# Turned left rows in the order (row, segment) instead of (segment, row), in a recurrent attention kernel with streamed weights

## The chip, the cores and the metric

The kernel runs on one core of a Trainium2 chip. The metric is the device time of one execution in microseconds. A core has a matrix engine (TensorE, PE in the profile, PEld for its weight loads), three engines for vector work (VectorE = DVE, ScalarE = ACT, GpSimd = POOL), and a queue engine (SyncE = SP). Transfers are carried out by 16 DMA engines; SP, ACT and POOL issue them.

## The reference

The input `x` has 2048 rows of 1024. It is normalized row by row (`xn`), and the result is `x` plus two branches. Branch A is attention with a recurrent memory, over 64 segments of 32 rows:

```
mem = mem0                                        # 8 rows
for s in range(64):
    h = concat([mem, xn[32*s : 32*s+32]])         # 40 rows
    q, k, v = h @ Wq, h @ Wk, h @ Wv              # 32 heads of 128
    p = softmax(mask(q k^T * scale))              # a key is seen from memory rows, or if it isn't later
    o = (p v) @ Wo
    mem = o[:8];  out[32*s : 32*s+32] = o[8:]
```

So the memory of a segment is made by the segment before, and the segments run one after the other. Branch B takes the two rows of `xn` with the highest score under `w_r`, sends them through a gated feed-forward layer (width 3584) and adds the result to these two rows. Data are bf16.

## The kernel before

**Weights.** Wq, Wk, Wv and Wo are cut into 64 granules of 512 KB. 44 stay in SBUF for the whole run. The other 20 are streamed anew in every segment: `fetch` (L346) issues on SP's queue, into five slots (tile `g`), from copies in DRAM (`wsc`) that the first segment makes. SP waits until TensorE has let go of a slot.

**Main rows and left rows.** A segment's tile has 32 rows. 24 of them are the segment's first 24 rows of x (XM = 24), the other 8 are the memory. The segment's last 8 rows (XL = 8, the *left* rows) do not fit. Four segments are a group `G`, and the left rows of its four segments, 4 x 8 = 32 rows, are one more tile `STL`. Their q, k and v need no memory, so they are computed for the next group while this group's segments run: each `left_pass` (L566) multiplies STL with a granule that happens to be there, into `PSl`. The places are written out by hand in `PASSES`, and the copies out of PSum in `COPIES`. Which of the 32 columns of STL is which row is the subject of the change: before it, column 8 s + r is row r of segment s.

**The way of the left rows.** `load_left` (L318) fetches them from x with four DMAs on GpSimd's queue, one for each quarter of the columns: into `XL`, `BX` (the next group's rows, normalized by `norm_left` with the statistics in `ML`) and, with `crossed`, into `OL` (the same rows again for the final sum, `sum_left`, L330). The left q and k of a group go to DRAM (`ql_d[G]`, four matrices of 128 x 512, L617 from ScalarE's queue), since each segment needs only its own quarter of the rows. `new_lx` (L481) fetches this quarter, 128 rows of 512, for the next segment, in the ninth step of the output projection (`w == 9`); `turn_lx` (L488) transposes it on TensorE behind the first transposes of the segment (L491), and ScalarE copies it into `QKL`. In the first segment `turn_first` (L497) does the same without DRAM.

**Softmax.** For each half of the heads, `soften` (L682) writes the normalized weights of the 32 main keys into PM and those of the 8 left keys into a tile with room for all 32 left rows of a group, zero at the other segments' (L704); VectorE transposes both in blocks of 32 x 32 (L706, L708), and `attend` (L712) multiplies them with VM and VL, the values of the main rows and of the left rows of the whole group. The room with zeros is slot 3 of `OTL` (`left_out`, L510) or a part of `BX`; `clear_pl` (L744) clears it with a memset on GpSimd.

**Statistics.** `spread` (L224) brings means and deviations from rows of 128 to the layouts that are needed, by matmuls with 0/1 matrices made at the start (`SELM`, `SELL`), once for the first 128 rows and once for the rest.

**Order.** The order on each engine is the order of the program (a manual schedule): hooks at (phase, step) in a segment place softmax, attend, loads and copies between the matmuls (L802 for q, k, v, L575 for the output projection).

Of the kernel before, what the change touches and what calls it, by code (L numbers as in the profile page):

```python
# [11 lines left out]
ALU = mybir.AluOpType  # L12
# [38 lines left out]
def kernel(  # L51
# [16 lines left out]
    nc = tc.nc  # L68
    P = 128
# [3 lines left out]
    SEG = int(A_seg_len)  # L73
# [4 lines left out]
    NT = S // P  # L78
# [4 lines left out]
    XM = SEG - M  # L83
    XL = M
    NK = M + SEG

    x2 = A_x[0]
# [38 lines left out]
    ql_d = [dram.tile([4, P, 512], BF16, name=f"ql_d{t}") for t in range(NT)]  # L126
# [22 lines left out]
    IDENT = const.tile([P, P], BF16, name="IDENT")  # L149
# [10 lines left out]
    BS = psS.tile([P, 512], F32, name="BS")  # L160
    BT = psT.tile([P, 512], F32, name="BT")
    SPS = BS[:, 0:8 * NK].rearrange("p (i a k) -> p i a k", i=4, a=2)
    PTB = BT[:, 0:256].bitcast(BF16)
    PTB2 = BT[:, 256:512].bitcast(BF16)
    OPB = BT[:, 256:256 + 4 * NK]
    MR = BS[:, 320:320 + 2 * NSEG].rearrange("p (s c) -> p s c", c=2)
    ML = BS[:, 448:448 + 2 * NT].rearrange("p (t c) -> p t c", c=2)
    nc.vector.memset(SPS[:, :, :, :], 0.0)
    for b in range(2):
        nc.vector.memset(X[b][:, :], 0.0)  # L170
# [3 lines left out]
    MISC = home(hm, [P, 2048], BF16, "MISC")  # L174
    SELM = MISC[:, 0:512].rearrange("p (s g r) -> p s g r", s=4, g=4)
    SELL = MISC[:, 512:640].rearrange("p (g s r) -> p g s r", g=4, s=4)
# [4 lines left out]
    RI16 = MISC[:, 728:792].bitcast(F32).rearrange("p (t c) -> p t c", c=2)  # L181
    RF = MISC[:, 792:824].bitcast(F32)
    MF = MISC[:, 824:824 + 2 * (XM + 1)].bitcast(F32)
    WRB = MISC[:, 1024:2048]
    nc.vector.memset(MF, 0.0)
    nc.vector.memset(MISC[:, 0:640], 0.0)

    for q0 in range(0, P, 32):
        for c0, c1, base, step in ((0, XM, 0, -1), (XM, XM + 1, -XM, 0)):
            nc.gpsimd.affine_select(out=MF[q0:q0 + 32, c0:c1], in_=MF[q0:q0 + 32, c0:c1], pattern=[[step, c1 - c0]],  # L190
                                    compare_op=ALU.is_ge, fill=NEG, base=base, channel_multiplier=1)
        nc.gpsimd.affine_select(out=CT[q0:q0 + 32, 14:15], in_=CT[q0:q0 + 32, 14:15], pattern=[[0, 1]],
                                compare_op=ALU.is_ge, fill=1.0, base=XM - 1, channel_multiplier=-1)
    nc.vector.tensor_scalar(out=KMSK, in0=NMSK, scalar1=-1.0, scalar2=1.0, op0=ALU.mult, op1=ALU.add)
    nc.vector.tensor_copy(out=MASK, in_=MF[:, 0:XM])
    nc.vector.tensor_copy(out=NEGR, in_=MF[:, XM:XM + 1])
    for s in range(4):
        nc.vector.tensor_copy(out=SELM[:, s, :, 0:XM],
                              in_=IDENT[:, 32 * s:32 * s + XM].unsqueeze(1).to_broadcast([P, 4, XM]))
        nc.vector.tensor_copy(out=SELL[:, s, :, :],  # L200
                              in_=IDENT.rearrange("p (s c) -> p s c", c=32)[:, :, XM:SEG])


    XP = {}
# [19 lines left out]
    def spread(t0, t1):  # L224

        n = t1 - t0
        sd_rows(MV[:, t0:t1, :], VE[:, t0:t1])
        PD = OPB
        for s in range(5):
            sel = SELM[:, s, :, :].rearrange("p g r -> p (g r)") if s < 4 else SELL.rearrange("p g s r -> p (g s r)")  # L230
            nc.tensor.matmul(PD[:, 32 * s:32 * s + 2 * n], lhsT=sel, rhs=MV[:, t0:t1, :].rearrange("p t c -> p (t c)"),
                             start=(s == 0), stop=True, skip_group_check=True)
        for s in range(4):
            mr = MR.rearrange("p (t s) c -> p t s c", s=4)[:, t0:t1, s, :]
            pd = PD[:, 32 * s:32 * s + 2 * n].rearrange("p (t c) -> p t c", c=2)
            nc.vector.tensor_copy(out=mr[:, :, 0], in_=pd[:, :, 0])
            nc.vector.tensor_scalar(out=mr[:, :, 1], in0=pd[:, :, 1], scalar1=NMSK, scalar2=None, op0=ALU.add)
        nc.vector.tensor_copy(out=ML[:, t0:t1, :], in_=PD[:, 128:128 + 2 * n].rearrange("p (t c) -> p t c", c=2))
        nc.vector.tensor_copy(out=RI16[:, t0:t1, 0], in_=MV[:, t0:t1, 0])
        nc.vector.reciprocal(out=RI16[:, t0:t1, 1], in_=MV[:, t0:t1, 1])  # L240

# [23 lines left out]
    def two_rows(m, tag):  # L265
        t = one.tile([P, 4], F32, tag=tag, name="RI")
        nc.vector.tensor_copy(out=t[:, 0:1], in_=m[:, 0:1])
        nc.vector.reciprocal(out=t[:, 1:2], in_=m[:, 1:2])
        return t
# [46 lines left out]
        nc.vector.tensor_copy(out=gview(st)[:, :, :, XM:SEG], in_=PTm[:, :, :, XM:SEG])  # L316

    def load_left(G, t, crossed=False):  # L318
        o4 = x2[4 * G * SEG:4 * (G + 1) * SEG, :].rearrange("(s r) d -> s r d", s=4)
        for g in range(4):  # L320
            b = 2 * (g % 2) + g // 2 if crossed else g
            nc.gpsimd.dma_start(out=t[32 * g:32 * (g + 1), :], in_=o4[:, XM:SEG, 256 * b:256 * (b + 1)])
        return t

    def norm_left(t, G):
        mr = two_rows(ML[:, G, :], "ri")
        nc.vector.tensor_scalar(out=t[:, :], in0=t[:, :], scalar1=mr[:, 0:1], scalar2=mr[:, 1:2],
                                op0=ALU.subtract, op1=ALU.mult)

    def sum_left(t, G):  # L330

        mr = two_rows(ML[:, G, :], "ri")
        nc.vector.tensor_scalar(out=mr[:, 0:1], in0=mr[:, 0:1], scalar1=mr[:, 1:2], scalar2=-1.0,
# [87 lines left out]
    load_x(0)  # L421
    nc.sync.dma_start(out=WRB, in_=B_w_r.unsqueeze(0).to_broadcast([P, D]))
    load_seg(0)
# [57 lines left out]
    def new_lx(s):  # L481
        t = lx[0] = one.tile([P, 512], BF16, tag="bA", name="LX")
        G, j = divmod(s, 4)
        nc.gpsimd.dma_start(out=t[:, :], in_=ql_d[G].rearrange("m (q s r) c -> (m q) s r c", q=4, s=4)[:, j])  # L484

    lx = [None]

# [9 lines left out]
    def turn_first(mat, half, XBl):  # L497
        if mat == 0 and half == 0:
            qkl[0] = one.tile([P, 4, 4, 4, XL], BF16, tag="bC", name="QKL")
        PTq = PTB.rearrange("p (i c) -> p i c", i=4)  # L500
        for il in range(4):
            nc.tensor.transpose(out=PTq[:, il, :], in_=XBl[:, il * P:(il + 1) * P], identity=IDENT[:, :])
        nc.scalar.copy(out=qkl[0][:, :, 2 * half + mat, :, :],
                       in_=PTB.rearrange("p (i q s r) -> p i q s r", i=4, q=4, s=4)[:, :, :, 0, :])

    qkl = [None]
    group = {}
# [113 lines left out]
    for s in range(NSEG):  # L621
        G, j = divmod(s, 4)
# [59 lines left out]
        def soften(half):  # L682
            S8 = SPS.rearrange("p i a k -> p (i a) k")
            DN = one.tile([P, 8], F32, tag="nm", name="DN")
            nc.vector.tensor_reduce(out=DN[:, :], in_=S8, axis=AX.X, op=ALU.add)
            nc.vector.reciprocal(out=DN[:, :], in_=DN[:, :])
            PT2 = one.tile([P, 2, 4, 64], BF16, tag=("bA", "bE")[half], name="PT2")
            PTm, PTl = PT2[:, 0], PT2[:, 1]
            PM = PTl.rearrange("p i q -> p (i q)").rearrange("p (b k) -> p b k", b=8)
            PLt = zeros_and_left()  # L690
            dnb = DN[:, :].unsqueeze(2)
            nc.vector.tensor_tensor(out=PM, in0=S8[:, :, 0:32], in1=dnb.to_broadcast([P, 8, 32]), op=ALU.mult)
            apart = half == 1 and j == 3
            if apart:
                OT[0] = one.tile([P, 640], BF16, tag="kt", name="OT")
                Z = OT[0][:, 512:640]
                nc.vector.memset(Z, 0.0)
                parts = [(slice(0, 4), Z.rearrange("p (b s r) -> p b s r", b=4, s=4)), (slice(4, 8), PLt[:, 4:8])]
                OT[0] = OT[0][:, 0:512].rearrange("p (i j r) -> p i j r", i=4, j=4)
            else:  # L700
                parts = [(slice(0, 8), PLt)]
            for bs, z in parts:
                n = bs.stop - bs.start
                nc.vector.tensor_tensor(out=z[:, :, j, :], in0=S8[:, bs, 32:NK],  # L704
                                        in1=dnb[:, bs].to_broadcast([P, n, XL]), op=ALU.mult)
            nc.vector.transpose(out=PTm.rearrange("p i q -> p (i q)"), in_=PM.rearrange("p b k -> p (b k)"))  # L706
            for bs, z in parts:
                nc.vector.transpose(out=PTl.rearrange("p i q -> p (i q)")[:, 32 * bs.start:32 * bs.stop],  # L708
                                    in_=z.rearrange("p b s r -> p (b s) r"))
            PTs[half] = (PTm, PTl)  # L710

        def attend(half, ph, turn_too=None):  # L712
# [26 lines left out]
        def zeros_and_left():  # L739

            z = left_out()[:, :, 3, :] if j or s == 0 else nxt["bx"][:, 0:256].rearrange("p (h r) -> p h r", r=XL)
            return z.rearrange("p (b s) r -> p b s r", s=4)

        def clear_pl():  # L744
            if j == 0 and s > 0:
                nxt["bx"] = one.tile([P, 512], BF16, tag=roles[0], name="BX")
            z = zeros_and_left()
            nc.gpsimd.memset(z[:, :, j - 1, :] if j > 1 else z, 0.0)

        def get_left():  # L750
            t = nxt["bx"] if s > 0 else one.tile([P, 512], BF16, tag=roles[0], name="XL")
# [42 lines left out]
        for p, (mat, half) in enumerate(PHASES):  # L794
# [3 lines left out]
            for kc in range(KC):  # L798
                g = 8 * p + kc
# [98 lines left out]
    ri = T2[0:2, 28:32].bitcast(F32)  # L898
# [99 lines left out]
```

## Time and profile before

| | us |
|---|---|
| three runs | 1884.78, 1889.17, 1875.67 |
| median | 1884.78 |
| profiled execution | 1878.39 |
| its span, first to last instruction | 1876.7 |

In the profiled execution TensorE is busy for 84% of the span, VectorE for 47%, ScalarE for 37%, GpSimd for 24%. 712.29 MB move through the DMA engines, 380 GB/s in the mean, and most of it are the streamed granules. The mean granted clock of TensorE is 0.957.

A line of the groups has the line of the kernel, the engine, the operation, what is written and read, a count, the busy time in us and the mean in ns, and the idle time of the engine just ahead of these instructions with what ended it. A line of the waits has the waiting engine and line, whom it waited for, the total in us, how often, and the longest. A line of a window has the time that each engine was busy in it, the granted clock, the share of DMA time and GB/s. A line of the timeline has start, duration and operation. The lines of DMA queues have packets, MB and the time of the packets as a share of 16 engines.

### The profile page before, as it was taken

What the parts mean: (1) busy time and instruction counts of PE and PEld (TensorE: products, weight loads), DVE (VectorE), ACT (ScalarE), POOL (GpSimd) and SP (SyncE); (2) the same over time, 40 slices, a digit from 0 to 9 for tenths busy, and PEclk for the clock granted to TensorE, in tenths of its full rate; (3) what the DMA queues carried; (4) which work ended last, traced back from release to release, by engine and by line L of the source; (5) the groups of instructions that cost most, each with busy time, mean ns of one, the idle gap of its engine ahead of it and who ended that gap; (6) DMA issues with size and microseconds to landing.
All of it is one profiled execution on the core that took longest, in us unless ns stands there. A gap on an engine that the chain in (4) does not pass through costs nothing.

```text
span 1876.7 us, 80489 instructions
## 1 busy us (share of the span) xinstructions
PE 1572.0 (84%) x34976; PEld 850.8 (45%) x34976; DVE 885.9 (47%) x2929; ACT 692.0 (37%) x1948; POOL 452.5 (24%) x898
## 2 busy tenths in 40 slices
PE   3458898889888988899889988988888888888864
PEld 1124444444454444445454444444444444444433
DVE  6725544544455444544454454544554454445430
ACT  1113433443344343444343344434343344334320
POOL 3111322213131322213131322323132221312120
PEclk8669999999999999999999999999999999999995
DMA  9999999999999999999999999999999999999998
GB/s 370 405 353 385 373 379 381 384 372 375 397 382 398 367 389 390 385 383 380 382 376 390 366 397 379 387 392 373 371 383 382 372 382 380 370 381 368 368 404 329
DMA packets 232115, 712.29 MB, mean 380 GB/s; under 512 B 39296, under 2 KB 53168, under 8 KB 231760
## 3 DMA queue, kind: packets, MB, share of 16 engines
q1 hardware_dynamic: 194384, 671.18, 93.4%
q0 software_dynamic: 28736, 28.09, 4.7%
q10 hardware_dynamic: 8640, 7.87, 1.2%
q8 instruction: 274, 4.49, 0.9%
q14 instruction: 81, 0.66, 0.1%
HBM read 694.32 MB, written 22.29 MB: 382 GB/s over the span
## 4 chain that ended last, share of the span: by engine, by line
DMA 57%; PE 37%; DVE 3%; issue 1%; ACT 1%; SPq 1%; ACTq 0%; DVEq 0%
DMA g<-wsc 50%; PE PSm L802 20%; PE PSl L568 5%; PE WO L575 4%; PE BT L638 3%; DMA XP<-in_A_x_dram 2%; PE WL L587 2%; DMA MW<-in_B_w_gate_dram 1%; DVE XR L248 1%; DMA MW<-in_B_w_up_dram 1%; DMA g<-in_A_Wq_dram 1%; DMA wres<-in_A_Wo_dram 1%; DMA g<-in_A_Wo_dram 1%; DMA MW<-in_B_w_down_dram 1%; DMA g<-in_B_w_down_dram 1%
## 5 line engine op out<-in xcount | busy, mean ns | idle before, releaser
L802 PE MATMUL PSm<-wres,ST 128*32 128x512 bf16 x8448 | 704.9, 384 | 7.8 <-DMA wres<-in_A_Wv_dram 3.6
L802 PEld LDWEIGHTS <-ST 128*32 128x32 bf16 x12288 | 323.0, 96 | 417.9 <-issue 174.7
L802 PE MATMUL PSm<-g,ST 128*32 128x512 bf16 x3588 | 361.4, 387 | 100.9 <-DMA g<-wsc 77.8
L575 PEld LDWEIGHTS <-OT 128*32 128x32 bf16 x8192 | 220.5, 97 | 162.8 <-issue 137.7
L821 ACT CAST XB<-PSm 128x512 bf16<-128x512 f32 x256 | 150.6, 588 | 293.2 <-PE PSm L802 290.9
L575 PE MATMUL WO<-wres,OT 128*32 128x256 bf16 x5632 | 238.6, 278 | 16.0 <-DMA wres<-in_A_Wo_dram 8.0
L484 POOL DMA_DIRECT2D LX<-ql_d x63 | 33.6, 533 | 816.0 <-PE WO L575 366.1
L575 PE MATMUL WO<-g,OT 128*32 128x256 bf16 x2560 | 132.7, 281 | 80.1 <-DMA g<-wsc 70.2
L568 PE MATMUL PSl<-wres,STL 128*32 128x512 bf16 x2112 | 184.0, 389 | 0.3 <-issue 0.2
L872 POOL DMA_DIRECT2D out_dram<-X x256 | 129.5, 513 | 215.0 <-DVE X L870 169.7
L653 DVE COPY KT<-BT 128x512 bf16<-128x512 bf16 x112 | 45.9, 410 | 286.5 <-issue 186.8
L273 POOL DMA_DIRECT2D X<-in_A_x_dram x256 | 129.5, 510 | 190.3 <-PE PSm L802 68.6
L378 ACT COPY BK<-KEPT 128x512 bf16<-128x512 bf16 x126 | 74.4, 590 | 130.0 <-PE WO L575 102.0
L646 ACT COPY QT<-BT 128x512 bf16<-128x512 bf16 x128 | 75.0, 586 | 125.9 <-PE BT L491 74.1
L638 PEld LDWEIGHTS <-XB 128*128 128x128 bf16 x1024 | 58.4, 98 | 117.8 <-ACT XB L821 67.9
L638 PE MATMUL BT<-IDENT,XB 128*128 128x128 bf16 x1024 | 102.0, 222 | 9.2 <-ACT XB L821 7.8
L568 PEld LDWEIGHTS <-STL 128*32 128x32 bf16 x3072 | 84.5, 98 | 55.7 <-issue 10.6
L870 DVE TENSOR_TENSOR X<-WO,X 128x256 bf16<-128x256 f32 x64 | 27.2, 425 | 170.4 <-PE WO L575 170.4
L831 ACT CAST VM<-PSm 128x512 bf16<-128x512 f32 x128 | 76.0, 594 | 85.0 <-PE PSm L802 83.8
L724 PEld LDWEIGHTS <-VM 32*128 32x128 bf16 x2048 | 65.5, 91 | 85.3 <-issue 72.2
L382 DVE COPY g<-KEPT 128x512 bf16<-128x512 bf16 x126 | 47.7, 420 | 108.5 <-PE PSm L802 62.0
L670 DVE TENSOR_TENSOR BS<-BS,CT 128x96 f32<-128x96 f32 (+1 forms) x256 | 59.1, 231 | 77.1 <-PE BS L663 72.7
(173 smaller groups left out, 2363.5 us busy)
## 6 DMA issues: line engine op xcount, KB each, us to landing
g<-wsc SPq DMA_DIRECT2D x1134, 512.0 KB, 6.1
g<-wsc SPq DMA_DIRECT2D x63, 256.0 KB, 5.5
LX<-ql_d POOLq DMA_DIRECT2D x63, 128.0 KB, 5.9
ql_d<-XBl ACTq DMA_DIRECT2D x60, 128.0 KB, 5.7
MW<-in_B_w_gate_dram SPq DMA_DIRECT2D x16, 448.0 KB, 9.5
MW<-in_B_w_up_dram SPq DMA_DIRECT2D x16, 448.0 KB, 9.0
wres<-in_A_Wk_dram SPq DMA_DIRECT2D x12, 512.0 KB, 11.6
MW<-in_B_w_down_dram SPq DMA_DIRECT2D x12, 512.0 KB, 10.6
```

The lines of the kernel that those rows point to most:

```text
L273: nc.gpsimd.dma_start(out=X[s % 2][32 * g:32 * g + XM, :], in_=x2[s * SEG:s * SEG + XM, 256 * g:256 * (g + 1)])
L378: copy(out=back[c][:, :], in_=KEPT_COLS[KEPT_WHOLE][c])
L568: nc.tensor.matmul(PSl[32 * jq:32 * jq + 32, :], lhsT=STL[:, g % KC, :], rhs=part(Gv, jq), start=first_, stop=last_, tile_position=(0, 32 ...
L575: nc.tensor.matmul(PS[32 * g:32 * g + 32, 0:256], lhsT=lhs(h), rhs=Gv[:, D * hs + 256 * g:D * hs + 256 * (g + 1)], start=(first and hs == ...
L638: nc.tensor.transpose(out=PTq[:, il, :, :].rearrange("p j r -> p (j r)"), in_=XB[:, il * P:(il + 1) * P], identity=IDENT[:, :])
L646: nc.scalar.copy(out=QT[half][:, :, :], in_=pv)
L670: nc.vector.tensor_tensor(out=S4, in0=S4, in1=m, op=ALU.add)
L724: nc.tensor.matmul(o, lhsT=VM[half][q0:q0 + 32, il * P:(il + 1) * P], rhs=PTm[q0:q0 + 32, il, 0:NK], start=True, stop=False, tile_position ...
L802: nc.tensor.matmul(PSm[32 * jq:32 * jq + 32, :], lhsT=ST[:, kc, :], rhs=part(Gv, jq), start=(kc == 0), stop=(kc == KC - 1), tile_position= ...
L821: nc.scalar.copy(out=XB[:, :], in_=PSm[:, :])
L831: nc.scalar.copy(out=VM[half][:, :], in_=PSm[:, :])
L872: nc.gpsimd.dma_start(out=out2[s * SEG:s * SEG + XM, 256 * g:256 * (g + 1)], in_=OB[32 * g:32 * g + XM, :])
```

## The change

The 32 left rows that go through STL now stand as column 4 r + s, row before segment. Everything that indexes them follows: the load of the left rows (except the crossed one for `OL`, which keeps its order), their statistics (a second matrix `SELR` and a second table `MLR`, since `sum_left` still uses `ML`), the slice of `ql_d` that `new_lx` loads, the copy in `turn_first`, and the place of the left weights in the room that soften writes and clear_pl clears. The output rows `OTL` keep (segment, row).

For `new_lx` the 128 source rows of one segment were 16 blocks of 8 neighbouring rows, 32 rows from block to block; now they are every fourth row of the 512. In soften, the 8 left weights of a head and segment were 8 neighbouring elements; now they stand 4 elements apart. The core of the diff:

```diff
+    MLR = BS[:, 480:480 + 2 * NT].rearrange("p (t c) -> p t c", c=2)
...
+    SELR = MISC[:, 888:888 + 128].rearrange("p (g r s) -> p g r s", g=4, r=XL)
...
+        nc.vector.tensor_copy(out=SELR[:, s, :, :],
+                              in_=IDENT.rearrange("p (s c) -> p c s", c=32)[:, XM:SEG, :])
...
-        PD = OPB
-        for s in range(5):
-            sel = SELM[:, s, :, :].rearrange("p g r -> p (g r)") if s < 4 else SELL.rearrange("p g s r -> p (g s r)")
+        PD = BT[:, 256:448]
+        for s in range(6):
+            if s < 4:
+                sel = SELM[:, s, :, :].rearrange("p g r -> p (g r)")
+            else:
+                sel = SELL.rearrange("p g s r -> p (g s r)") if s == 4 else SELR.rearrange("p g r s -> p (g r s)")
...
-        nc.vector.tensor_copy(out=ML[:, t0:t1, :], in_=PD[:, 128:128 + 2 * n].rearrange("p (t c) -> p t c", c=2))
+        for m, at in ((ML, 128), (MLR, 160)):
+            nc.vector.tensor_copy(out=m[:, t0:t1, :], in_=PD[:, at:at + 2 * n].rearrange("p (t c) -> p t c", c=2))
...
     def load_left(G, t, crossed=False):
-        o4 = x2[4 * G * SEG:4 * (G + 1) * SEG, :].rearrange("(s r) d -> s r d", s=4)
+
+        o4 = x2[4 * G * SEG:4 * (G + 1) * SEG, :].rearrange("(s r) d -> s r d", s=4)[:, XM:SEG, :]
+        if not crossed:
+            o4 = o4.rearrange("s r d -> r s d")
         for g in range(4):
             b = 2 * (g % 2) + g // 2 if crossed else g
-            nc.gpsimd.dma_start(out=t[32 * g:32 * (g + 1), :], in_=o4[:, XM:SEG, 256 * b:256 * (b + 1)])
+            nc.gpsimd.dma_start(out=t[32 * g:32 * (g + 1), :], in_=o4[:, :, 256 * b:256 * (b + 1)])
...
-        mr = two_rows(ML[:, G, :], "ri")
+        mr = two_rows(MLR[:, G, :], "ri")
...
-        nc.gpsimd.dma_start(out=t[:, :], in_=ql_d[G].rearrange("m (q s r) c -> (m q) s r c", q=4, s=4)[:, j])
+        nc.gpsimd.dma_start(out=t[:, :], in_=ql_d[G].rearrange("m (x s) c -> (m x) s c", s=4)[:, j])
...
-                       in_=PTB.rearrange("p (i q s r) -> p i q s r", i=4, q=4, s=4)[:, :, :, 0, :])
+                       in_=PTB.rearrange("p (i q r s) -> p i q r s", i=4, q=4, s=4)[:, :, :, :, 0])
...
-                nc.vector.tensor_tensor(out=z[:, :, j, :], in0=S8[:, bs, 32:NK],
-                                        in1=dnb[:, bs].to_broadcast([P, n, XL]), op=ALU.mult)
+                nc.vector.tensor_tensor(out=z[:, :, :, :, j],
+                                        in0=S8[:, bs, 32:NK].rearrange("p b (h x) -> p b h x", h=4),
+                                        in1=dnb[:, bs].unsqueeze(3).to_broadcast([P, n, 4, 2]), op=ALU.mult)
...
-                                    in_=z.rearrange("p b s r -> p (b s) r"))
+                                    in_=z.rearrange("p b h x s -> p (b h) (x s)"))
...
-            nc.gpsimd.memset(z[:, :, j - 1, :] if j > 1 else z, 0.0)
+            if j > 1:
+                nc.gpsimd.memset(z[:, :, :, :, j - 1], 0.0)
+            else:
+                nc.gpsimd.memset(z.rearrange("p b h x s -> p (b h) (x s)"), 0.0)
```

More of the change, by code (lines that the diff above doesn't have):

```diff
@@ L697, in soften @@
                 nc.vector.memset(Z, 0.0)
-                parts = [(slice(0, 4), Z.rearrange("p (b s r) -> p b s r", b=4, s=4)), (slice(4, 8), PLt[:, 4:8])]
+                parts = [(slice(0, 4), Z.rearrange("p (b h x s) -> p b h x s", b=4, h=4, s=4)), (slice(4, 8), PLt[:, 4:8])]
                 OT[0] = OT[0][:, 0:512].rearrange("p (i j r) -> p i j r", i=4, j=4)
@@ L741, in zeros_and_left @@
             z = left_out()[:, :, 3, :] if j or s == 0 else nxt["bx"][:, 0:256].rearrange("p (h r) -> p h r", r=XL)
-            return z.rearrange("p (b s) r -> p b s r", s=4)
+            return z.rearrange("p (b h) (x s) -> p b h x s", h=4, s=4)
         def clear_pl():
```

## Prediction

> **What bounds the kernel now.** First the page: busy shares, then the DMA queues.
>
> ```profile
> span 1876.7 us, 80489 instructions
> PE 1572.0 (84%) x34976; PEld 850.8 (45%) x34976; DVE 885.9 (47%) x2929; ACT 692.0 (37%) x1948; POOL 452.5 (24%) x898
> ...
> q1 hardware_dynamic: 194384, 671.18, 93.4%
> q0 software_dynamic: 28736, 28.09, 4.7%
> q10 hardware_dynamic: 8640, 7.87, 1.2%
> q8 instruction: 274, 4.49, 0.9%
> ```
>
> The last column is the time of a queue's packets as a share of 16 engines' span. The four add up to 100.2%: the DMA engines are full from end to end, with the weights (q1) taking 93.4 of it. TensorE is 84% busy. Second, the waits of TensorE and of SP's queue, which say who follows whom.
>
> ```profile
> PE PSm L802 <- DMA g<-wsc: 77.8, 170, 2.3
> PE WO L575 <- DMA g<-wsc: 70.2, 145, 1.7
> ```
> ```profile
> SPq L355 <- PE PSm L802: 448.1, 656, 4.1
> SPq L355 <- DMA g<-wsc: 385.3, 740, 2.6
> ```
>
> TensorE's long waits are for streamed weights, and SP waits for TensorE to free one of five slots, but by then several granules are in flight (one lands 6.1 us after its issue, and 1134 in some 1700 us is one every 1.5 us), so the engines below stay full all the same.
>
> ```profile
> g<-wsc SPq DMA_DIRECT2D x1134, 512.0 KB, 6.1
> ```
>
> So the time is what the DMA engines need for their packets: a change is worth what it takes from that, or what it makes the engines stand still. Third, therefore, the rate in the stretches that the change touches. LX's packets begin some 3.5 us after its issue. I asked for the windows 1.5 to 3.0 us behind each of the 58 issues of LX between 200 and 1760 us (just ahead of its packets), and for those 3.75 to 5.25 us behind it (with them). First and last row of each 58; the last column is GB/s, the one before it the DMA share:
>
> ```profile
> 210.98:212.48 1.50, 1.50 (x38) 0.75 (x34) 0.43 (x1) 0.59 (x1) 1.50 (x4) 1.00 1.04 382
> ...
> 1734.94:1736.44 1.50, 0.84 (x24) 0.64 (x24) 0.00 (x0) 0.00 (x0) 0.00 (x0) 1.00 1.03 418
> ```
> ```profile
> 213.23:214.73 1.50, 0.07 (x6) 0.07 (x7) 0.00 (x0) 0.00 (x0) 0.72 (x2) 1.00 0.98 325
> ...
> 1737.19:1738.69 1.50, 0.62 (x13) 0.23 (x10) 0.88 (x3) 0.59 (x1) 0.61 (x2) 0.96 1.03 382
> ```
>
> Over the 58 rows the share is 1.02 in both, but the rate is 390 GB/s ahead of LX and 356 with it: the engines are as busy and move less. That is all that this load costs beyond its bytes.
>
> **The change part by part.** *The load of LX (L484, 63 times, 128 KB).* Before, the source is 16 blocks of 8 rows that lie together; after, 128 rows of 1 KB, 4 KB apart. Bytes, the length of a run (1 KB) and the number of partitions stay. Its price now, from one window that holds LX alone on q0, and, for a load of short runs that stand 2 KB apart, from one with BX and X (left and main rows of x, 64 + 48 KB):
>
> ```profile
> q1 hardware_dynamic: 175, 0.63, 86.9%
> q0 software_dynamic: 47, 0.13, 17.3%
> ```
> ```profile
> q1 hardware_dynamic: 630, 2.03, 90.5%
> q0 software_dynamic: 278, 0.13, 8.2%
> ```
>
> The first is 931.9 to 934.0 us: 17.3% of 2.1 us is 0.363 us of all 16 engines for one LX (131 KB). The second is 962.5 to 968.4 us: 8.2% of 5.9 us is 0.484 us for 115 KB, 1.52 times as much for a byte. If LX comes to cost what those scattered rows cost, it takes 0.363 x 1.52 = 0.55 us, 0.19 us more, times 63 = **+11.9 us**. The best that it can gain is that its stretch runs at the highest rate that I find, a stretch of whole granules and copies:
>
> ```profile
> 40.00:44.00 4.00, 0.00 (x0) 0.00 (x0) 2.92 (x6) 0.00 (x0) 3.65 (x8) 0.77 1.04 421
> ```
>
> (1 - 356/421) x 1.5 us x 63 = **-14.6 us**; if the dip alone goes, (1 - 356/390) x 1.5 x 63 = **-8.2 us**. Of the rows the nearest to the new shape is LX itself (same bytes, run and partitions), which says 0; what pulls it down is that source and destination now walk all 128 partitions in one stride, as the weights' do. I take a third of the dip, **-3 us**, and keep -14.6 and +11.9.
>
> *Its landing.* A later LX would hold up the transposes of L491, and TensorE behind them:
>
> ```profile
> 928.80 0.53 POOL L484 DMA_DIRECT2D LX<-ql_d  x1 [14.93 <-PE WO L575]
> ...
> 936.33 0.39 PE L491 MATMUL BT<-IDENT,LX 128*128 128x128 bf16 x4
> ```
> ```profile
> L484 POOL DMA_DIRECT2D LX<-ql_d x63: 528/528/549, 120.1 to 1787.4; - x63
> ...
> DMA to landing us min/median/max: 4.3/5.9/7.1
> ```
>
> The need comes 7.5 us behind the issue here, the landing 5.9 in the median, and no wait of TensorE for LX is in the list. 0; behind L484 on GpSimd stand the stores of the segment's rows (L872), which nobody awaits within the segment. Its issue stays near 0.53 us.
>
> *The load of the left rows (L322, 64 of its 128 DMAs; those of OL keep their order).* The outer dimension is 8 rows instead of 4 segments; bytes and 512 B runs stay. The worst stretch with BX and X in it:
>
> ```profile
> 966.00:968.00 2.00, 2.00 (x48) 0.92 (x44) 0.74 (x4) 0.47 (x2) 0.73 (x3) 1.00 0.89 311
> ```
>
> Against 390 GB/s that is (1 - 311/390) x 2 us = 0.4 us, in 15 groups 6 us: bounds **-6 and +6 us**; the nearest row is the load itself, so 0. [...]
>
> *Vector work.* L704 writes its 64 left weights in runs of 2 with a step of 4, not in runs of 8; L748's memset likewise; the transposes (L708) read what they read before. The nearest rows are these operations themselves:
>
> ```profile
> L704 DVE TENSOR_TENSOR OTL<-BS,DN 128x64 bf16<-128x64 f32 x98 | 20.5, 209 | 0.0
> ```
> ```profile
> 923.71 0.21 DVE L704 TENSOR_TENSOR OTL<-BS,DN 128x64 bf16<-128x64 f32 x1
> ...
> 924.31 0.45 DVE L708 STREAM_TRANSPOSE PT<-OTL 128x256 bf16<-128x256 bf16 x1
> ```
> ```profile
> 926.62 0.19 PE L724 MATMUL BS<-PT,VM 32*128 32x40 bf16 x1
> ```
>
> Same elements, so 0.21 us again; were it twice that, 0.21 us more in each of two softmaxes, 0.42 us x 63 = 26 us without cover. The cover: L708 ends at 924.76 and TensorE, busy with the output projection, comes to use it at 926.62, 1.86 us later. 0, with 0 to +26 if that cover were gone. The memset is short, and
>
> ```profile
> L748 POOL MEMSET OTL<- 128x256 bf16 x17 | 5.6, 329 | 0.0
> L748 POOL MEMSET OTL<- 128x64 bf16 x32 | 5.4, 170 | 0.0
> ```
>
> stands in a queue that sits idle before every LX, 14.93 us in the row above: 0.
>
> *Setup.* Four copies into SELR, a sixth small matmul and one copy into MLR, twice.
>
> ```profile
> 13.47 0.34 DVE L327 TENSOR_SCALAR XL<-XL,RI 128x256 bf16<-128x256 bf16 x1 [4.05 <-DMA XL<-in_A_x_dram]
> ```
> ```profile
> L200 DVE COPY MISC<-IDENT 128x32 bf16<-128x32 bf16 x4 | 0.7, 173 | 0.0
> ```
> ```profile
> L238 DVE COPY BS<-BT 128x30 f32<-128x30 f32 x1 | 0.2, 197 | 0.0
> ```
>
> 0.7 us and two times 0.2 us. The first part ends before DVE's wait of 4.05 us for XL, which hides it; the second is in the first segment, with the engines full. 0, bound +1.1 us.
>
> **Sum.** The profiled execution took 1878.39 us (its span is 1.7 less): 1878.4 - 3 = 1875.4. The three runs' median, 1884.78, is 6.4 us above that execution, which makes it 1881.8 from there; I put the forecast between the two, at **1879 us**: no difference that can be told. One per cent, 18.8 us, is about what a measurement of this kernel can tell from no change.
>
> **The rivals.** *It does nothing.* LX's own price stays 0.363 us and the dip stays: 1878 to 1885. For it speaks that bytes and runs are the same and that all engines are as full in the dip as ahead of it. *Full gain.* Both dips go, LX's to the best rate (-14.6) and the left loads' (-6): 1878.4 - 20.6 = 1858, faster by 1.1%. For it speaks that the dip comes exactly with LX's packets at an unchanged share, so packets get in each other's way; against it that the left rows' other half, OL, is untouched. [...] *Scattered reads.* After, every 1 KB that LX reads stands 4 KB from the next, where 8 KB lay together. If these reads are slow, the price is that of the scattered rows, +0.19 us, and the weights beside them fall to the worst rate too, (1 - 311/356) x 1.5 us = 0.19 us: 0.38 us x 63 = +24 us, 1902, slower by 1.3%. For it: BX and X cost 1.52 times as much for a byte and have the lowest rates. Against it: their runs are half as long, and they go to 32 and 24 partitions, not 128. It decides from 0.30 us for each LX on, that is when LX and what it does to its neighbours cost 1.8 times its 0.363 us. [...] *The strided write is slow* (L704): below 1.86 us more nothing comes of it, above that it would show as TensorE's wait at L724, up to the 26 us: 1904.
>
> **How the numbers follow.** Forecast of a small gain 0.34; nothing 0.20; full gain 0.18; scattered reads 0.25, of which 0.05 without the neighbours' part, at +11.9 us, within a per cent; slow write 0.03. So faster 0.18, same 0.34 + 0.20 + 0.05 = 0.59, slower 0.20 + 0.03 = 0.23. The range reaches from the full gain, 1857, to the scattered reads and a little beyond, 1903; the forecast's own is 1864 (the dip and the left loads' 6 us gone from 1878.4) to 1891 (+11.9).
>
> **What would show it.** In the profile after, the 58 windows with LX should have 360 to 380 GB/s instead of 356 (390 or more for the full gain, under 340 for scattered reads), q0's share in a window that holds LX alone should give 0.33 to 0.40 us (0.55 for scattered reads), the landing should stay within 5 to 7 us, L704 at 0.21 us and L484 near 0.53 us, and no wait of TensorE for LX or for L708 should appear. The prediction is wrong if the time moves by over 1%, or if it stays while one of these moves and another takes it back.

## The result and the profile after

| | median (lowest to highest), us | ratio, 95% interval | profiled execution, us |
|---|---|---|---|
| before, 7 runs | 1883.77 (1875.67 to 1889.17) | 1 | 1878.39 |
| after, 7 runs | 1866.46 (1858.72 to 1873.31) | 0.9914 [0.9884, 0.9943] | 1871.24 |

The changed kernel is 0.9% faster: 16 us, between 11 and 22. The two profiled executions stand only 7.15 us apart, because the one of before is 5.4 us under its median and the one of after 4.8 us over its own. So the two traces show where the time went, and the medians how much it was.

The page of the changed kernel, first part and DMA queues:

```profile
span 1869.5 us, 80499 instructions
PE 1565.6 (84%) x34978; PEld 851.4 (46%) x34978; DVE 886.3 (47%) x2935; ACT 692.7 (37%) x1948; POOL 455.8 (24%) x898
...
DMA packets 232115, 712.27 MB, mean 381 GB/s; under 512 B 39040, under 2 KB 52912, under 8 KB 231760
...
q1 hardware_dynamic: 194384, 671.18, 93.0%
q0 software_dynamic: 28736, 28.08, 4.7%
q10 hardware_dynamic: 8640, 7.87, 1.2%
q8 instruction: 274, 4.49, 0.9%
```

Every engine does about what it did, as many packets move as many bytes but for 0.02 MB, and the shares still add up to 99.8%. The page alone doesn't show what became shorter. Neither do the waits of TensorE and of SP's queue, which still follow each other around the weights:

```profile
PE PSm L817 <- DMA g<-wsc: 77.0, 167, 2.0
PE WO L586 <- DMA g<-wsc: 66.3, 135, 1.7
```
```profile
SPq L366 <- PE PSm L817: 434.9, 652, 3.5
SPq L366 <- DMA g<-wsc: 377.4, 700, 2.0
```

The windows around LX do. First, a middle one and the last of the 59 windows 3.75 to 5.25 us behind LX's issue, in the trace of after (the last column is GB/s, the one before it the DMA share):

```profile
212.07:213.57 1.50, 1.10 (x24) 0.45 (x19) 0.00 (x0) 0.00 (x0) 0.76 (x2) 1.00 1.03 355
...
936.34:937.84 1.50, 1.50 (x30) 0.66 (x32) 0.53 (x2) 0.00 (x0) 1.50 (x4) 1.00 1.02 418
...
1757.80:1759.30 1.50, 1.03 (x20) 0.42 (x13) 0.76 (x2) 0.57 (x1) 0.75 (x3) 1.00 0.83 306
```

Single windows scatter widely (306 to 418 here), so only the means count. Before, the rate was 390 GB/s ahead of LX and 356 with it. After, it is 376 ahead and 389 with it: the dip (the lower rate at an unchanged DMA share) is gone. A smaller step is in the 2 us that follow (5.25 to 7.25 us behind the issue), first in the trace of before, then of after:

```profile
214.73:216.73 2.00, 2.00 (x40) 1.13 (x43) 0.56 (x2) 0.07 (x1) 1.00 (x3) 1.00 1.01 365
...
1738.69:1740.69 2.00, 2.00 (x24) 0.84 (x20) 0.07 (x1) 0.00 (x0) 1.75 (x4) 0.50 1.02 406
```
```profile
213.57:215.57 2.00, 1.21 (x24) 0.57 (x20) 0.76 (x2) 0.59 (x1) 1.30 (x3) 1.00 1.01 385
...
1759.30:1761.30 2.00, 0.45 (x10) 0.23 (x11) 0.00 (x0) 0.01 (x1) 0.00 (x0) 1.00 1.02 413
```

The means of these rows (58 and 59) are 383 and 395 GB/s. Both steps together are (1 - 356/389) x 1.5 + (1 - 383/395) x 2 = 0.127 + 0.061 = 0.188 us for each LX, 11.8 us for 63. The windows ahead of LX go the other way, 376 GB/s for 390, and take back (1 - 376/390) x 1.5 = 0.054 us, 3.4 us for 63; so the three windows together show 8.4 us of the 16. A window of after that holds one LX alone on q0, 909.7 to 911.6 us:

```profile
q1 hardware_dynamic: 183, 0.66, 85.3%
q0 software_dynamic: 47, 0.13, 17.2%
```

17.2% of 1.9 us is 0.327 us, where it was 0.363. The 0.363 was a dear one, however: over the windows 2.9 to 5.9 us behind the issue in which q0 moves 0.13 MB, that is LX and hardly anything else, the median is 0.342 us before (35 windows) and 0.327 after (37). LX's own packets became hardly cheaper (0.015 us, 1 us for 63); by the rates above, what became faster is what moves beside them. Of the other rows, the group of LX's issues on GpSimd, its landing, the listing of DMA issues, and the two strided writes:

```profile
L495 POOL DMA_DIRECT2D LX<-ql_d x63 | 35.3, 560 | 819.6 <-PE WO L586 380.6 <-DVE OT L745 283.6 <-ACT OTL L747 118.7
...
L715 DVE TENSOR_TENSOR OTL<-BS,DN 128x64 bf16<-128x64 f32 x82 | 23.7, 288 | 0.0
...
L761 POOL MEMSET OTL<- 128x64 bf16 x32 | 8.3, 261 | 0.0
```
```profile
DMA to landing us min/median/max: 4.8/5.8/6.6
```

The landing stayed (5.8 us for 5.9) and the issue takes 560 ns for 533. The softmax's product L704 (now L715) went from 214 to 288 ns in this group, whose row before, without the smaller shapes that the 209 ns of the prediction have mixed in, is this; the memset went from 170 to 261.

```profile
L704 DVE TENSOR_TENSOR OTL<-BS,DN 128x64 bf16<-128x64 f32 x82 | 17.6, 214 | 0.0
```

### The profile page after: what moved, and what is told of

It reads as the page before. It is cut to its first block, busy times and chain, and to the rows that moved or that the text cites. A ratio compares the mean times of both kernels' runs of the same rounds, so it can differ in the third digit from the quotient of the medians.

```text
span 1869.5 us, 80499 instructions
## 1 busy us (share of the span) xinstructions
PE 1565.6 (84%) x34978; PEld 851.4 (46%) x34978; DVE 886.3 (47%) x2935; ACT 692.7 (37%) x1948; POOL 455.8 (24%) x898
## 4 chain that ended last, share of the span: by engine, by line
DMA 58%; PE 35%; DVE 4%; issue 2%; SPq 1%; ACT 1%; POOL 0%; DVEq 0%; POOLq 0%; ACTq 0%
DMA g<-wsc 50%; PE PSm L817 18%; PE WO L586 5%; PE PSl L579 4%; PE BT L649 2%; DMA XP<-in_A_x_dram 2%; PE WL L598 2%; DMA MW<-in_B_w_up_dram 1%; DVE XR L256 1%; DMA MW<-in_B_w_gate_dram 1%; DMA g<-in_A_Wq_dram 1%; DMA wres<-in_A_Wo_dram 1%; DMA g<-in_B_w_down_dram 1%; PE BT L301 1%; DMA out_dram<-X 1%
## 5 line engine op out<-in xcount | busy, mean ns | idle before, releaser
L579 PEld LDWEIGHTS <-STL 128*32 128x32 bf16 x3072 | 84.5, 98 | 57.3 <-issue 11.9
L745 DVE CAST OT<-BT 128x128 bf16<-128x128 f32 x128 | 37.2, 291 | 126.7 <-PE BT L301 71.6
L745 ACT CAST OT<-BS 128x128 bf16<-128x128 f32 x128 | 34.1, 266 | 166.0 <-PE BT L738 89.7
## 6 DMA issues: line engine op xcount, KB each, us to landing
wres<-in_A_Wk_dram SPq DMA_DIRECT2D x12, 512.0 KB, 11.9
```

The lines of the kernel that those rows point to most:

```text
L579: nc.tensor.matmul(PSl[32 * jq:32 * jq + 32, :], lhsT=STL[:, g % KC, :], rhs=part(Gv, jq), start=first_, stop=last_, tile_position=(0, 32 ...
L745: copy(out=OT[half][:, 2 * ph + jl, :, :], in_=ov[:, :, 0:SEG])
```

## The experiments

The theory going in: the gain is LX's alone, and it comes from the way it walks its 128 partitions, since one stride over all 128 is what the weights' loads have too. The rivals: it comes from the other parts (left loads, softmax), or from where LX's rows lie in memory. Each ratio is to the kernel before, measured beside it.

### The changed kernel again

No edit.

> The changed kernel once more, beside the others of this call. Ratio to the kernel before 0.988 to 0.994 (0.9914 was measured). In the 1.5 us with LX's packets (3.75 to 5.25 us behind its issue) 385 to 392 GB/s, as in the first profile after the change (389); the kernel before has 356 there.

1868.36 us against 1881.29: 0.994 [0.9917, 0.9963]. The windows give 383 GB/s ahead of LX and 393 with it. The gain and the missing dip are there again; the two measurements put the gain at 0.6 to 0.9%. The 2 us behind have 393 GB/s, so by the same sum the three windows show 10 us here.

### Both kernels without LX

The load of LX is replaced in both kernels by a memset of its tile, so the transposes turn zeros.

```diff
-        nc.gpsimd.dma_start(out=t[:, :], in_=ql_d[G]...[:, j])
+        nc.gpsimd.memset(t[:, :], 0.0)
```

> The kernel before without the 63 loads of LX: a memset of the tile on GpSimd stands in their place, so the left queries and keys of all but the first segment are zero. What LX costs before: 63 x (0.363 + 0.13) = 31 us by its own share and the dip, ratio 0.983. If LX costs no more than its bytes at 412 GB/s: 20 us, ratio 0.989.

> The changed kernel without the 63 loads of LX, in the same way (the left queries and keys of all but the first segment are zero). If LX alone makes the gain, nothing else of the change counts and this takes the same as the kernel before without LX (within 3 us); the changed kernel's LX then costs some 20 us, ratio 0.980 to 0.983. If the left loads make the gain, this one is 8 to 16 us below the kernel before without LX.

Before without LX 1852.15 us, 0.985 [0.982, 0.9881]; after without LX 1852.62, 0.9861 [0.9826, 0.9896]. Without this load the two kernels take the same time: 0.0011 apart, 2 us, with some 9 us of uncertainty. So what the change gains goes through LX, and the left loads, the softmax and the setup together count for nothing that can be told here. In the windows 3.75 to 5.25 us behind the memset both kernels have 398 GB/s in the mean, so the dip to 356 belongs to LX. The same runs price LX: 28 us of time before (22 to 34), and after, from 0.9861 to 0.9914 or 0.994, some 10 to 15 us, each with 8 to 9 us of uncertainty, where some 20 us were expected for after. The difference, 13 to 18 us, is the gain over again, less those 2 us, and no second measure of it.

### LX's source in one piece

After, but `ql_d` is stored segment by segment, so that the 128 KB of LX lie together; the stores take the scattering.

```diff
+    def unit_rows(G, m):
+        return ql_d[G][:, 32 * m:32 * (m + 1), :].rearrange("s x c -> x s c")
...
-        nc.gpsimd.dma_start(out=t[:, :], in_=ql_d[G].rearrange("m (x s) c -> (m x) s c", s=4)[:, j])
+        nc.gpsimd.dma_start(out=t[:, :], in_=ql_d[G][j])
...
-            stores.append(lambda: nc.scalar.dma_start(out=ql_d[Gu][2 * half + "qk".index(u[0])], in_=XBl[:, :]))
+            stores.append(lambda: nc.scalar.dma_start(out=unit_rows(Gu, 2 * half + "qk".index(u[0])), in_=XBl[:, :]))
...
```

> The changed kernel, but the left q and k are stored so that a segment's 128 rows lie together: LX reads 128 KB in one piece, still in one stride of 128; the stores go out in 32 x 4 rows. If the form makes the gain: no dip with LX (385 to 392 GB/s), ratio 0.990 to 0.995 (the stores may get a dip of their own). If it is the spread of the reads over DRAM: the dip comes back or deepens, 340 to 362 GB/s, ratio 0.996 to 1.003.

1868.69 us, 0.9922 [0.9895, 0.9949]. First and last of 59 windows with LX:

```profile
213.20:214.70 1.50, 0.76 (x16) 0.33 (x12) 0.43 (x2) 0.00 (x0) 1.27 (x3) 1.00 1.02 402
...
1754.97:1756.47 1.50, 0.80 (x10) 0.36 (x14) 0.81 (x3) 0.49 (x1) 0.92 (x2) 0.79 1.02 418
```

Mean 390 GB/s, 381 ahead: no dip, and no difference to after that can be told (0.994 beside it). Reading rows 4 KB apart or rows that lie together makes no difference here, so the place of the reads is not the cause.

### LX in 16 blocks of 8 again

After, but LX is loaded in a 16 x 8 form, and the order is put right behind the transposes: first by ScalarE's copy into QKL, then, in a second kernel, by the identity that TensorE reads in the transposes.

```diff
-        nc.gpsimd.dma_start(out=t[:, :], in_=...[:, j])
+        nc.gpsimd.dma_start(out=t[:, :], in_=...[:, j].rearrange("(b a) c -> a b c", a=16))
...
-        nc.scalar.copy(out=t.rearrange("p i m q r -> p (i m q r)"), in_=PTB2)
+        nc.scalar.copy(out=t.rearrange("p i m q r -> p i (m q r)").rearrange("p i (b a) -> p i a b", a=16),
+                       in_=PTB2.rearrange("p (i a b) -> p i a b", i=4, a=16))
```

> The changed kernel, but LX is loaded in 16 x 8 instead of one stride of 128: the same 128 source rows, 4 KB apart, into partitions in another order, which ScalarE's copy into QKL puts right. The left loads, the softmax and all else stay as changed. If the form of the transfer makes the gain: the dip comes back, 350 to 362 GB/s in the 1.5 us with LX, and the ratio to before is 0.995 to 1.000. If the place of the reads in DRAM makes it: no dip, 385 to 392 GB/s, ratio 0.991. If the left loads from x make it: a dip as before, but the ratio stays at 0.991 to 0.993.

1951.73 us, 1.0375 [1.0345, 1.0405], far more than LX could cost. The row of ScalarE's copy, after and then here:

```profile
L506 ACT COPY QKL<-BT 128x512 bf16<-128x512 bf16 x63 | 37.3, 591 | 0.0
```
```profile
L506 ACT COPY QKL<-BT 128x512 bf16<-128x512 bf16 x63 | 152.4, 2420 | 0.0
```

The helper takes 1.83 us more in each segment, 115 us of ScalarE in all, and the kernel is 83 us slower than after. The dip is back (374 GB/s ahead, 344 with LX), but by time this kernel decides nothing. Its page does teach something on the share:

```profile
DMA packets 232115, 712.27 MB, mean 364 GB/s; under 512 B 39040, under 2 KB 52912, under 8 KB 231760
...
q1 hardware_dynamic: 194384, 671.18, 92.0%
q0 software_dynamic: 28736, 28.08, 4.6%
```

The span is 86 us longer than after's, something else holds the work up, and q1's share still reads 92.0 where it was 93.0; the four largest queues add up to 98.7%. So the share hardly falls when the rate does, 364 GB/s against 381: a full share is no proof that the DMA engines set the time.

The second helper:

```diff
-            nc.tensor.transpose(out=PTq[:, il, :], in_=lx[0][:, il * P:(il + 1) * P], identity=IDENT[:, :])
+            nc.tensor.matmul(PTq[:, il, :], lhsT=lx[0][:, il * P:(il + 1) * P], rhs=IDENT[:, :].rearrange("p (a b) -> p b a", a=16),
+                             is_transpose=True, start=True, stop=True)
```

> Again the changed kernel with LX loaded in 16 x 8, but the order is put right by the identity that TensorE's transposes read (columns with a step), and ScalarE's copy into QKL is the changed kernel's. If the 70 us of the first try were ScalarE's copy with a step (2.42 us instead of 0.59): the time falls to 0.994 to 1.002 of the kernel before, L506 takes 0.59 us, and the dip stays, 335 to 362 GB/s in the 1.5 us with LX. If the 16 x 8 load itself cost them: 1.03 or more again.

1916.45 us, 1.0189 [1.0154, 1.0224]; the windows give 386 GB/s ahead and 353 with LX, which is the dip of before. First and last of 57 with LX:

```profile
217.00:218.50 1.50, 0.88 (x20) 0.48 (x19) 0.17 (x1) 0.00 (x0) 0.99 (x2) 1.00 0.93 325
...
1744.44:1745.94 1.50, 1.50 (x33) 0.50 (x26) 0.79 (x3) 0.47 (x1) 0.94 (x2) 1.00 0.94 312
```

The transposes of LX, after and then here:

```profile
L502 PE MATMUL BT<-IDENT,LX 128*128 128x128 bf16 x252 | 24.3, 219 | 0.0
```
```profile
L502 PE MATMUL BT<-IDENT,LX 128*128 128x128 bf16 x252 | 67.3, 401 | 0.0
```

L506 takes 592 ns again and 35 us are won back, but again the helper was dearer than expected, 43 us more of TensorE. The kernel is about 50 us slower than after; with the 43 us and the 12 us that the windows give for the dip that is about accounted for, but only if TensorE's delay is paid in full. So these two kernels show that the 16 x 8 form brings the dip; they don't show what the dip costs.

### The kernel before with LX in one stride

Before, with LX stored as it will be read: each matrix of left q or k goes out in four stores instead of one.

```diff
+    def store_unit(engine, G, m, X):
+        to = ql_d[G].rearrange("s (m q r) c -> m q s r c", m=4, q=4)[m]
+        for q in range(4):
+            engine.dma_start(out=to[q], in_=X[32 * q:32 * (q + 1), :])
...
-        nc.gpsimd.dma_start(out=t[:, :], in_=ql_d[G].rearrange("m (q s r) c -> (m q) s r c", q=4, s=4)[:, j])
+        nc.gpsimd.dma_start(out=t[:, :], in_=ql_d[G][j])
...
```

> The kernel before with one part of the change alone: left rows stay (segment, row), the left loads and the softmax too, but the left q and k are stored segment by segment (four DMAs for each store instead of one), so that LX is one stride of 128 partitions. If LX's form makes the gain: no dip (385 to 395 GB/s), ratio 0.990 to 0.996. If the left loads or the softmax have made it: ratio 0.998 to 1.002.

1957.4 us, 1.0416 [1.0383, 1.0449]. The rate doesn't dip with LX (359 GB/s ahead, 375 with it), though it is below the 385 to 395 expected, and the four stores in place of one cost far more than LX gave. The shares of its chain, and a wait for these stores:

```profile
DMA 49%; PE 33%; ACTq 6%; ACT 6%; DVE 3%; issue 3%; SPq 1%; POOL 0%; DVEq 0%
```
```profile
ACT QT L651 <- DMA ql_d<-XBl: 66.0, 25, 3.2
```

Its time decides nothing on the gain. That a kernel with the left loads and the softmax of before loses the dip goes with the theory, but with the whole kernel slower this is a weak sign.

### Two halves: by partitions, or by columns

This pair asks whether "one stride" is what counts. Both are after with LX in two DMAs of 64 KB. In the one each takes 64 partitions, still with one stride; in the other each takes all 128 partitions and half the columns. Issues and bytes are the same; the runs are 1 KB in the first and 512 B in the second.

```diff
+        src = ql_d[G].rearrange("m (x s) c -> (m x) s c", s=4)[:, j]
+        for h in range(2):
+            nc.gpsimd.dma_start(out=t[64 * h:64 * (h + 1), :], in_=src[64 * h:64 * (h + 1), :])
```
```diff
+            nc.gpsimd.dma_start(out=t[:, 256 * h:256 * (h + 1)], in_=src[:, 256 * h:256 * (h + 1)])
```

Each of them in a single run:

> The changed kernel, LX in two DMAs of 64 partitions each, one stride in each. If any single stride will do: no dip, 380 to 392 GB/s in the 1.5 us with LX. If the 128 partitions must be dealt out to the engines as those of the weights are: a part of the dip comes back, 362 to 375 GB/s.

> The changed kernel, LX in two DMAs of all 128 partitions and half of the columns each (runs of 512 B): the control for the two DMAs of 64 partitions. No dip with either theory, 380 to 392 GB/s; if the shorter runs count, 370 to 380.

1880.91 us by partitions, with 385 GB/s ahead and 342 with LX; 1869.73 us by columns, with 384 and 386. The dip by partitions is deeper than the 362 to 375 expected. Then with twelve runs each:

> LX in two DMAs of 64 partitions, one stride in each, now timed. If the dealing of 128 partitions to the engines makes the gain, this gives it back, though each DMA has one stride: dip 333 to 362 GB/s, ratio 0.997 to 1.002. If one stride is what counts: ratio 0.991 to 0.994.

> The control with two DMAs of all 128 partitions and half of the columns, now timed: ratio 0.991 to 0.995 with either theory, no dip; 0.997 or more if two DMAs or runs of 512 B cost anything.

By partitions 1889.85 us, 1.0044 [1.0023, 1.0066]; by columns 1874.26 us, 0.9953 [0.9927, 0.9979]. First and last of 59 windows with LX, first by partitions, then by columns:

```profile
213.32:214.82 1.50, 0.20 (x3) 0.00 (x0) 0.29 (x1) 0.00 (x0) 0.76 (x2) 1.00 1.02 355
...
1754.08:1755.58 1.50, 1.15 (x22) 0.54 (x22) 0.52 (x2) 0.04 (x1) 1.36 (x3) 1.00 1.05 358
```
```profile
214.55:216.05 1.50, 1.39 (x22) 0.36 (x24) 0.52 (x2) 0.00 (x0) 1.07 (x2) 1.00 1.03 410
...
1745.57:1747.07 1.50, 1.50 (x36) 0.74 (x29) 0.24 (x2) 0.00 (x0) 1.50 (x4) 1.00 0.91 339
```

The means are 382 GB/s ahead and 341 with LX by partitions, 382 and 386 by columns. The two differ in how the partitions are shared out and in the length of the runs, and the shorter runs are on the side without the dip; the issues, the bytes, the source and the packets in each size class of the page (233124 in all, 40048 under 512 B) are the same. By partitions the dip comes back, and with it 0.9%, 16 us, as much as the whole gain; this form is even slower than the kernel before and than the 1.002 expected. So one stride is not enough: of the forms tried, those without a dip are the ones in which each transfer covers all 128 partitions in one stride.

### All left rows as (row, segment)

After, with `OTL` and the load and store of `OL` in the new order too.

```diff
-            group["otl"] = one.tile([P, H, 4, XL], BF16, tag="otl", name="OTL")
+            group["otl"] = one.tile([P, H, XL, 4], BF16, tag="otl", name="OTL")
...
-        if not crossed:
-            o4 = o4.rearrange("s r d -> r s d")
+        o4 = o4.rearrange("s r d -> r s d")
...
```

> The changed kernel, and the rest of the left rows is turned to (row, segment) too: the output rows OTL, the second load of x for the sum (OL) and the store of the left rows have 8 rows outside instead of 4 segments. If the left loads have a part in the gain: 3 to 6 us less than the changed kernel, ratio 0.988. If only LX has: the same as the changed kernel within 2 us, ratio 0.991.

1863.16 us, 0.9915 [0.9882, 0.9947]. It is the lowest median of the kernels that load LX, 5 us under the changed kernel measured beside it (0.994), but the intervals overlap; whether it is better, and so whether the left loads have a small part, stays open. Its windows give 390 GB/s ahead and 387 with LX. Here the left weights are written still further apart:

```profile
L715 DVE TENSOR_TENSOR OTL<-BS,DN 128x64 bf16<-128x64 f32 x82 | 34.9, 425 | 0.0
...
L761 POOL MEMSET OTL<- 128x64 bf16 x32 | 13.1, 410 | 0.0
```

## Why the prediction was right, and where it wasn't

**The place and the sign** were right: the forecast's gain rested on the dip behind LX's issue, and the dip went. The prediction's test line for it was "360 to 380 GB/s instead of 356 (390 or more for the full gain)"; 389 and, again, 393 came, which is the full gain's side of the line. The time, 1866, lies between the forecast, 1879, and the full gain, 1858: within the 1% that stood for no difference, but by the interval a gain. From a median of 1883.8 the forecast's -3 us would have been 1881, and the full gain's -20.6 us 1863. So the full gain, which had a chance of 0.18, came nearer than the forecast, and that "no difference" held is luck: 0.9% is just under the 1%.

**The step that failed** is the size of LX's term: "Of the rows the nearest to the new shape is LX itself (same bytes, run and partitions), which says 0 ... I take a third of the dip, **-3 us**". It measured -8 to -12 us by the windows (-11.8 from the two behind the issue, -8.4 with the one ahead of LX in the sum), and by time the whole gain, -16 us (-11 to -22), since without LX the two kernels are equal to within 9 us; what the windows leave over is not placed. The prediction named what had changed, that "source and destination now walk all 128 partitions in one stride, as the weights' do", but gave it little weight beside bytes, run and number of partitions. The halves show that this is what mattered: with half the partitions in each transfer the rate with LX is 341, with all of them 386, at the same bytes and packets. The nearer rows were the weights' own loads, in whose windows 390 GB/s stood. What the term left out besides is the 2 us behind the window (0.061 us of 0.188), where the rate also rose.

**The full gain** was half right. The dip went as it said, but its LX part, -14.6, was worked out with a best rate of 421 GB/s, and 389 to 393 came, which in that window is the dip alone, -8.2; that the time came near is not due to that rate. Its part from the left loads (-6) shows no sign: without LX both kernels take the same, and the interval, -7 to +11 us, just holds it. Why the form of the transfer makes the dip is not shown: the profile doesn't say which DMA engine wrote which partition, so the dealing to the engines that two expectations suppose stays a supposition. What is shown is the pattern: a dip in 16 x 8 (344 to 356 GB/s with LX) and in 64 + 64 (341 and 342), none where each transfer covers all 128 partitions in one stride (386 to 393; in the slower kernel with four stores 375, with 359 ahead). Two partition halves took 1.0044 of the kernel before, one transfer 0.9914 and 0.994.

**Scattered reads** (0.25) fell: the 4 KB pitch costs nothing that can be told beside one piece (0.994 and 0.9922), and LX takes 0.327 us, not 0.55. The 0.55 rested on a misreading, too: the window with BX and X has 0.13 MB on q0 in its row, as LX's has, and not 115 KB (stores of `out_dram` are in it as well), which makes a byte 1.33 times as dear, not 1.52, and the +11.9 us some 63 x 0.12 = 7.6. The upper end of the forecast's own range, 1878.4 + 11.9, is 1890 and not 1891; nothing hangs on that.

**L704** was put at "0.21 us again" and takes 0.288; the memset takes 261 ns for 170, the issue 560 for 533. "Same elements" was no ground: with another spacing the same elements took longer. It cost nothing that can be told (without LX the two kernels are equal), as the extra 0.07 us is far below the cover of 1.86 us. TensorE's list of waits now has this line:

```profile
PE BS L672 <- DVE BX L715: 2.9, 13, 0.2
```

It can't be put down to the change: the kernel before without LX, whose product is written in the old order, has such a line as well:

```profile
PE BS L661 <- DVE BX L704: 3.3, 15, 0.2
```

**"So the time is what the DMA engines need for their packets"** was too simple. With ScalarE's stepped copy the kernel took 83 us longer at the same bytes, though the engines still read 98.7% full; and of the 43 us of TensorE in the 16 x 8 transposes most seem to have been paid as well. (LX's packets take 63 x 0.327 = 20.6 us of all engines after, and the load costs 10 to 15 us of time; but the uncertainty of these, 8 to 9 us, reaches 20.6.) So a share near 100% didn't say that no packet could have been moved sooner; the rate in GB/s was the column that told.

## What to carry to other kernels

Where DMA shares read full, compare the rate in windows ahead of a transfer and with it: a dip at the same share can be time that the shape of that transfer takes from its neighbours, as here (356 GB/s for 390, both at a share of 1.02), where it was won back without moving fewer bytes. To judge by this case, load a 128-partition tile beside a running stream in one transfer with one stride over all 128 partitions (0.9914 and 0.994 of the kernel before); if the source's order stands against that, change the order in which it is stored, and split by columns (0.9953) rather than by partitions (1.0044). Price the helper that puts the order right before the gain: the two tried here took 115 and 43 us of their engines, for a gain of 16.

## What the hardware showed that was not expected

Where 2-byte elements stood apart instead of next to each other, an operation took longer on each of four engines. VectorE's product of 64 elements takes 214 ns in runs of 8, 288 in pairs of elements 8 bytes apart (after), and 425 with every element 32 bytes from the next (all left rows); GpSimd's memset 170, 261 and 410. ScalarE's copy of 512 elements goes from 591 to 2420 ns when its output steps by 32 bytes, and TensorE's 128 x 128 transpose from 219 to 401 ns when the identity is read at a step of 16 bytes. The length of the runs changes with the spacing, so the two are not told apart.
